# Turning q and k by TensorE's transposes in the first eight steps of a fused RetNet and MLP kernel, with the heads paired anew and w_in's rows loaded to match

## The chip, the cores and the metric

The kernel runs on one core of a Trainium2 chip. Its time is what the device records for one execution, in microseconds (us), and a lower one is better. Medians of several executions are given. A comparison of two kernels uses runs on the same chip, taken in turns, and only runs in the fast state; all runs below were in it, but for m1_probe, which ran once and has no known state. Engines are written as in the profile: PE is TensorE's matmuls, PEld its weight loads, DVE is VectorE, ACT is ScalarE, POOL is GpSimd, SP is SyncE. The DMA engines are 16.

The kernel before takes 682.3 to 688.7 us from one execution to another. So effects below 2 us need the intervals that are given with them.

## The reference

```python
# attention: batch 4, 8 heads, 768 tokens, head_dim 64, float32
for t in range(S):
    state = gamma[None, :, None, None] * state + einsum('bhd,bhe->bhde', k[:, :, t], v[:, :, t])
    y[:, :, t] = scale * einsum('bhd,bhde->bhe', q[:, :, t], state)
x = y.transpose(0, 2, 1, 3).reshape(3072, 512)      # feature = head * 64 + d
h = x @ w_in                                        # 512 x 2048
g = h * (1.0 / (1.0 + exp(-1.702 * h)))
out = g @ w_out                                     # 2048 x 512
```

The weights reach the kernel as 64-bit floats and are narrowed on the chip: ScalarE and VectorE read both words of each.

## The kernel before

The recurrence runs in chunks of 64 tokens for two batches at a time: 24 steps. The first eight stand in a hand-written order between the narrowing of the weights and the first layer of the MLP. The other 16 turn q and k on VectorE and are not touched in substance. Here is what the change touches, cut.

```python
# loads of w_in: P = 128 partitions, two 512 KB transfers per pair of blocks
w1v = moe_w_in.bitcast(U32).rearrange("(c p) (f two) -> p c f two", p=P, two=2)
SRC = [w1v[:, 2 * h:2 * h + 2, 2 * p * P:2 * (p + 1) * P] for p in range(NP) for h in range(2)] + ...
def fetch(i):
    x = raw(i).rearrange("p (n two) -> p n two", two=2)
    pin(sp.dma_start(x.rearrange("p (c f) two -> p c f two", c=2) if i < NFF else x, SRC[i]))

def turn(j):                        # q and k of step j: from token rows to head_dim rows
    ...
    for n in (1, 0) if j else (0, 1):
        for s in range(HP):         # HP = 4
            for r in range(2):      # head HP * r + s goes to half r of the partitions
                pe.matmul(p[n][HALF[r], s, :], x[n][:, HP * r + s, :], ident, start=True, stop=True)

def attend(j, f=None):              # quarter-array matmuls (64 rows x 64 columns), four at a time
    ...                             # k q^T -> pa; k^T v -> pa; state and attention -> py

def aged(f):                        # state times the decay of a whole chunk, on ScalarE
    for s in range(HP):
        pin(act.activation(new[:, :, s], old[:, :, s], AF.Copy, scale=whole[:, s:s + 1]))

def lay_whole():                    # whole[half r, s] = decay of head HP * r + s
    for r in range(2):
        pin(pool.dma_start(whole[HALF[r]], bass.AP(..., offset=... + H + HP * r, ap=[[0, D], [1, HP]])))
```

The kernel lays four quarter-array matmuls (64 rows x 64 columns) side by side in the array, so that the two that share rows have different columns (in the trace, four of them begin within 20 ns at 21.24 us, and the next four 59 ns after the first). To keep that, a head's half of the partitions as an input (r) and as an output (o) are chosen independently of each other. Before, r parted the heads into 0 to 3 and 4 to 7, and o into even and odd ones. Even and odd heads in the halves of the output make chunk c of x's features the rows 128c to 128c + 127 of w_in, which are contiguous.

## Time and profile before

| | before |
|---|---|
| time, median of the first 4 runs | 684.62 us (684.2 to 684.91) |
| TensorE busy | 668.9 of 683.3 us |
| turns | 256 matmul records, 1.90 us each turn |
| w_in's transfers | 16 of 512 KB, 6.0 us from issue to landing in the median |

The prediction shows the page's main lines; these are further ones. First the view by windows: each row gives a stretch in us, the busy time of each engine with its instruction count, then TensorE's granted clock, the mean share of the DMA engines and GB/s.

```profile
10.00:20.00 10.00, 8.21 (x188) 5.96 (x187) 8.15 (x14) 9.11 (x29) 2.83 (x4) 1.00 0.89 231
20.00:30.00 10.00, 8.61 (x189) 7.43 (x186) 9.35 (x13) 8.00 (x26) 0.00 (x0) 1.00 0.87 227
...
40.00:50.00 10.00, 10.00 (x110) 8.61 (x104) 8.96 (x12) 7.39 (x22) 0.00 (x0) 1.00 0.91 241
```

The clock is whole (1.00; its record begins at 10.8 us, and the view counts time without a record as whole). The view of waits of the first 100 us (total, times, longest):

```profile
ACT W L189 <- DMA W<-in_moe_w_in_dram: 10.5, 4, 5.7
...
ACT W L189 <- DMA G<-in_moe_w_in_dram: 1.7, 2, 1.0
```

(Part of w_in passes through a buffer that the program calls G.) ScalarE's timeline has the wait for the whole decay, and the view of that tile the time of its load:

```profile
18.76 1.28 ACT L322 ACTIVATE state<-state,whole 128x128 f32<-128x128 f32 x4 [0.44 <-DMA whole<-in_col_decay_dram]
```

```profile
DMA to landing us min/median/max: 3.5/3.6/3.6
```

Last, the row of the page for the queue that brings instructions (transfers, MB, share), and two lines of TensorE's timeline.

```profile
24.72 0.45 PE L265 MATMUL pa<-G 64*64 64x64 f32 x12 [1.35 <-issue]
...
85.97 10.46 PE L396 MATMUL ph<-W,W 128*128 128x512 f32 x24
```

The 1.35 us without a cause was the one such wait above 0.4 us here, and it was not looked into before predicting. The group at 85.97 is the first of the second quarter of the MLP's first layer; its start will serve as a milestone.

### The profile page before, as it was taken

Reading aid. Unit: us, or ns where it says so; the run is one execution under the profiler, and the core shown is the slowest. Engines: PE = TensorE matmul, PEld = TensorE weight load, DVE = VectorE, ACT = ScalarE, POOL = GpSimd, SP = SyncE. Lnnn points to the kernel's source line nnn. Section 1 sums busy time; section 2 is a strip of 40 time slices with the busy share of each in tenths; the row PEclk is TensorE's granted clock in tenths of the full one; section 3 lists DMA queues with packets and bytes.
Section 4 is the critical chain, followed back from the end, with each engine's and each line's share of the span. In section 5 each row is a group of like instructions: output and inputs, shape, how many; then the busy total and the mean of one; then the engine's idle time right before and its main releaser. Section 6 shows DMA issues by size and latency. Waiting matters only on the chain.

```text
span 683.3 us, 13882 instructions
## 1 busy us (share of the span) xinstructions
PE 668.9 (98%) x5830; PEld 558.7 (82%) x5830; DVE 367.1 (54%) x514; ACT 151.1 (22%) x293; POOL 125.5 (18%) x116
## 2 busy tenths in 40 slices
PE   6899999999999999999999999999999999999997
PEld 4788854757788888888888888888888888888886
DVE  3899994989811843443752453563345372345241
ACT  5775423221000001332000332000333000233000
POOL 3000000000467414000434000244100243000030
PEclk9999999999999999999999999999999999999999
DMA  7887631332222224301333310313310210000001
GB/s 179 231 236 212 177 130 62 123 84 35 49 34 64 61 45 103 58 1 16 73 57 84 54 32 9 75 31 89 72 40 3 50 45 32 16 0 1 16 0 47
DMA packets 140334, 46.55 MB, mean 68 GB/s; under 512 B 131824, under 2 KB 132848, under 8 KB 140272
## 3 DMA queue, kind: packets, MB, share of 16 engines
q1 hardware_dynamic: 136352, 39.10, 24.9%
q0 software_dynamic: 1760, 5.26, 2.0%
q10 hardware_dynamic: 2160, 1.31, 0.6%
q8 instruction: 46, 0.75, 0.5%
q14 instruction: 16, 0.13, 0.1%
HBM read 39.33 MB, written 6.29 MB: 67 GB/s over the span
## 4 chain that ended last, share of the span: by engine, by line
PE 84%; DVE 7%; SPq 5%; DMA 1%; issue 1%; ACT 1%; ACTq 0%
PE pd L503 37%; PE px L435 16%; PE py L435 12%; PE ph L384 6%; SPq L140 4%; PE ph L396 4%; PE pa L265 2%; PE pt L232 2%; PE py L290 2%; PE pa L275 2%; PE py L284 2%; SPq L126 1%; PE pd L488 1%; DVE G L425 1%; DMA W<-in_moe_w_out_dram 1%
## 5 line engine op out<-in xcount | busy, mean ns | idle before, releaser
L503 PE MATMUL pd<-W,G 128*128 128x256 f32 x1088 | 240.5, 381 | 1.3 <-issue 0.9
L503 PEld LDWEIGHTS pd<-W,G 128*128 128x128 f32 x1088 | 205.2, 190 | 30.4 <-DVE G L426 1.2
L435 PE MATMUL px<-X,W 128*128 128x256 f32 x512 | 119.0, 379 | 0.0
L435 PEld LDWEIGHTS px<-X,W 128*128 128x128 f32 x512 | 97.3, 190 | 13.2
L435 PE MATMUL py<-X,W 128*128 128x256 f32 x384 | 90.7, 379 | 0.0
L435 PEld LDWEIGHTS py<-X,W 128*128 128x128 f32 x384 | 73.0, 190 | 9.9
L384 PE MATMUL ph<-X,W 128*128 128x256 f32 x256 | 57.6, 382 | 0.0
L396 PE MATMUL ph<-W,W 128*128 128x512 f32 x128 | 55.6, 592 | 0.0
L384 PEld LDWEIGHTS ph<-X,W 128*128 128x128 f32 x256 | 48.1, 190 | 8.2 <-issue 1.0
L256 POOL TENSOR_TENSOR kd<-kn_in,cold 128x512 f32<-128x512 f32 x14 | 16.4, 1173 | 187.5 <-PE pa L275 163.8
L396 PEld LDWEIGHTS ph<-W,W 128*128 128x128 f32 x128 | 24.3, 190 | 28.9 <-issue 28.4
L427 POOL TENSOR_TENSOR G<-G 128x512 f32<-128x512 f32 x20 | 29.5, 1480 | 91.8 <-DVE G L426 91.8
L356 ACT ACTIVATE sg<-G 128x512 f32<-128x512 f32 x48 | 30.3, 630 | 51.3 <-DVE G L445 31.0
L361 DVE TENSOR_TENSOR G<-G,sg 128x512 f32<-128x512 f32 x48 | 33.5, 699 | 13.7 <-ACT sg L356 13.7
L296 DVE TENSOR_TENSOR at<-pa,mask 128x512 f32<-128x512 f32 x16 | 11.0, 686 | 54.7 <-PE pa L275 54.7
L324 POOL TENSOR_TENSOR state<-state,whole 128x512 f32<-128x512 f32 x13 | 13.5, 1038 | 128.1 <-DVE state L332 127.9
L503 PE MATMUL pd<-W,W 128*128 128x256 f32 x160 | 35.8, 381 | 1.0 <-DVE W L426 1.0
L503 PEld LDWEIGHTS pd<-W,W 128*128 128x128 f32 x160 | 30.2, 190 | 6.3 <-DVE W L426 1.8
L475 ACT ACTIVATE u<-pd 128x512 f32<-128x512 f32 x6 | 3.6, 597 | 137.3 <-PE pd L503 137.3
L356 ACT ACTIVATE sg<-ph 128x512 f32<-128x512 f32 x32 | 18.9, 595 | 66.2 <-PE ph L396 32.9
L480 POOL DMA_DIRECT2D out_dram<-o x20 | 14.9, 745 | 91.4 <-DVE o L479 91.4
L445 DVE TENSOR_TENSOR G<-py,p 128x512 f32<-128x512 f32 x16 | 11.1, 692 | 38.1 <-PE py L435 38.1
(112 smaller groups left out, 676.0 us busy)
## 6 DMA issues: line engine op xcount, KB each, us to landing
W<-in_moe_w_in_dram SPq DMA_DIRECT2D x12, 512.0 KB, 6.1
v_in<-in_v_dram SPq DMA_DIRECT2D x48, 128.0 KB, 3.3
kn_in<-in_k_dram SPq DMA_DIRECT2D x42, 128.0 KB, 3.4
W<-in_moe_w_out_dram SPq DMA_DIRECT2D x10, 512.0 KB, 4.4
out_dram<-o POOLq DMA_DIRECT2D x20, 256.0 KB, 2.7
q_sq<-in_q_dram SPq DMA_DIRECT2D x256, 16.0 KB, 1.9
k_sq<-in_k_dram SPq DMA_DIRECT2D x256, 16.0 KB, 1.9
G<-in_moe_w_out_dram SPq DMA_DIRECT2D x6, 512.0 KB, 3.9
```

The source lines that it names most:

```text
L140: tc.keep_in_program_order(sp.dma_start(t[r0:r0 + C4, :, n], src[b + n * C4 // D, h0:h0 + HP, t0:t0 + C4, d0:d0 + C4] .rearrange("h p d -> ...
L232: pe.matmul(p[n][HALF[r], s, :], x[n][:, HP * r + s, :], ident, start=True, stop=True)
L256: pool.tensor_mul(KD[j], x, d.to_broadcast([P, H, D]))
L265: pe.matmul(pa[HALF[i], r, 0, s, :], KT[j][HALF[r], s, HALF[i]], QT[j][HALF[r], s, HALF[i]], start=True, stop=True)
L356: pin(act.activation(s, h, AF.Sigmoid, scale=1.702))
L361: pin(dve.tensor_mul(g, h[:, i], s[:, i]))
L384: pe.matmul(h[:, ab], w, X[:, 2 * th + c // 2, c % 2, :], start=(ab == 0 and c == 0), stop=(c == 3), skip_group_check=True)
L396: pe.matmul(h, w, X1[:, c // 2:4:2, c % 2, :], start=(c == 0), stop=(c == 3))
L427: pool.tensor_sub(a[1], a[1], a[0])
L435: pe.matmul(acc[:, u, :], W1[:, 2 * d + u, sa, c, :], X[:, sb, c, :], start=(start and u == 0 and c == 0), stop=(stop and c == 1), skip_gr ...
L480: (pool if m < NB - 1 else act).dma_start(rows[th, e], o)
L503: pe.matmul(p0[:, n, :], g1(m, p, sa)[:, n * P:(n + 1) * P], W2[:, sb, p, :], start=(new and p == 0 and n == 0), stop=(last and p == NP - ...
```

## The change

The intent is to halve TensorE's time for the turns of the first eight steps: one transpose of a 128 x 128 tile takes the place of two matmuls with 64 rows of result. The two heads of a tile are neighbours in memory, 2s and 2s + 1. Thus r now parts even and odd heads, o has to part 0 to 3 and 4 to 7, and the state, the mask, the row decay and the outputs follow. A chunk of x's features then has 64 rows of w_in from each half of the heads, 256 rows apart. The author loads each half of the partitions by a transfer of its own. The core of the diff:

```diff
-                    for r in range(2):
-                        pe.matmul(p[n][HALF[r], s, :], x[n][:, HP * r + s, :], ident, start=True, stop=True)
+                    pe.transpose(p[n][:, s, :], x[n][:, 2 * s:2 * s + 2, :].rearrange("p r d -> p (r d)"), ident)
...
-    w1v = moe_w_in.bitcast(U32).rearrange("(c p) (f two) -> p c f two", p=P, two=2)
+    w1v = moe_w_in.bitcast(U32).rearrange("(o c d) (f two) -> o d c f two", o=2, d=D, two=2)
...
-        x = raw(i).rearrange("p (n two) -> p n two", two=2)
-        pin(sp.dma_start(x.rearrange("p (c f) two -> p c f two", c=2) if i < NFF else x, SRC[i]))
+        if i < NFF:
+            f = slice(i // 2 * 2 * P, (i // 2 + 1) * 2 * P)
+            for o in range(2) if i < 2 else [i % 2]:
+                x, c = (raw(i), slice(2 * i, 2 * i + 2)) if i < 2 else (raw(i - i % 2, 2), slice(0, HP))
+                pin(sp.dma_start(x[HALF[o]].rearrange("p (c f two) -> p c f two", two=2, f=2 * P), w1v[o][:, c, f]))
...
-                        pe.matmul(pa[HALF[r], i, 1, s, :], kd[HALF[i], HP * r + s, :], vn[HALF[i], HP * r + s, :],
+                        pe.matmul(pa[HALF[r], i, 1, s, :], kd[HALF[i], 2 * s + r, :], vn[HALF[i], 2 * s + r, :],
...
-                            pe.matmul(py[HALF[o], r, 1, i, s2 * D:(s2 + 1) * D], old[HALF[r], i, 2 * s2 + o, :],
-                                      qt[HALF[r], 2 * s2 + o, HALF[i]], start=True, stop=True)
+                            pe.matmul(py[HALF[o], r, 1, i, s2 * D:(s2 + 1) * D], old[HALF[r], i, 2 * o + s2, :],
+                                      qt[HALF[r], 2 * o + s2, HALF[i]], start=True, stop=True)
...   (mask, row decay, outputs, gathers of q and k: the same instructions with other strides)
-                whole[HALF[r]], bass.AP(tensor=col_decay.tensor, offset=col_decay.offset + (D - 1) * W + H + HP * r,
-                                        ap=[[0, D], [1, HP]])))
+                whole[HALF[r]], bass.AP(tensor=col_decay.tensor, offset=col_decay.offset + (D - 1) * W + H + r,
+                                        ap=[[0, D], [2, HP]])))
```

More of the change, by code (lines that the diff above doesn't have):

```diff
@@ L103 @@
     state = [const.tile([P, 2, HP, D], F32, name=f"state{i}") for i in range(2)]
+    HALF = [slice(i * D, (i + 1) * D) for i in range(2)]
     ordered = [True]
@@ L136, in load @@
                 for r0 in range(0, P, C4):
-                    d0, h0 = r0 % D, r0 // D * HP
+                    d0, r = r0 % D, r0 // D
                     for n in range(P // C4):
@@ L140, in load @@
                         tc.keep_in_program_order(sp.dma_start(
-                            t[r0:r0 + C4, :, n], src[b + n * C4 // D, h0:h0 + HP, t0:t0 + C4, d0:d0 + C4]
+                            t[r0:r0 + C4, :, n], src[b + n * C4 // D, r:H:2, t0:t0 + C4, d0:d0 + C4]
                             .rearrange("h p d -> p h d")))
@@ L153 @@
             for r in (W2[:, 4], W2[:, 5], G[:, 6:8].rearrange("p a s t -> p a (s t)"))]
-    SRC = [w1v[:, 2 * h:2 * h + 2, 2 * p * P:2 * (p + 1) * P] for p in range(NP) for h in range(2)] \
-        + [w2v[:, f] for f in range(NFF)]
     def raw(i, n=1):
@@ L161, in fetch @@
     def fetch(i):
-        x = raw(i).rearrange("p (n two) -> p n two", two=2)
-        pin(sp.dma_start(x.rearrange("p (c f) two -> p c f two", c=2) if i < NFF else x, SRC[i]))
+        if i < NFF:
[3 more added lines that the diff above has]
+                pin(sp.dma_start(x[HALF[o]].rearrange("p (c f two) -> p c f two", two=2, f=2 * P), w1v[o][:, c, f]))
+        else:
+            pin(sp.dma_start(raw(i).rearrange("p (n two) -> p n two", two=2), w2v[:, i - NFF]))
     class Narrow:
@@ L209 @@
     QT, KT, KD, AT, TURNED, PA, PU, PY, SHARE = [{} for _ in range(9)]
-    HALF = [slice(i * D, (i + 1) * D) for i in range(2)]
     TWO = [(i, r) for i in range(2) for r in range(2)]
@@ L288, in attend @@
                     for i, o in TWO:
-                        s = 2 * s2 + o
-                        pe.matmul(py[HALF[o], i, 0, r, s2 * D:(s2 + 1) * D], vn[HALF[i], HP * r + s, :],
+                        s = 2 * o + s2
+                        pe.matmul(py[HALF[o], i, 0, s2, r * D:(r + 1) * D], vn[HALF[i], 2 * s + r, :],
                                   a[HALF[i], r, s, :], start=True, stop=True)
@@ L298, in by_state @@
     def by_state(f):
-        SHARE[f] = tmp = two.tile([P, 2, 2, P], F32, name="tmp", bufs=1)
-        pin(dve.tensor_mul(tmp, PY[f][:, :, 1].rearrange("p r i t -> p i r t"),
-                           rowd.rearrange("p (r s) t -> p r (s t)", r=2)[:, None].to_broadcast([P, 2, 2, P])))
+        SHARE[f] = tmp = two.tile([P, 2, 2, 2, D], F32, name="tmp", bufs=1)
+        pin(dve.tensor_mul(tmp, PY[f][:, :, 1].rearrange("p r i (s t) -> p i s r t", t=D),
+                           rowd.rearrange("p (s r) t -> p s r t", r=2)[:, None].to_broadcast([P, 2, 2, 2, D])))
     def output(f):
@@ L307, in output @@
         x = X1 if f // CB == 1 else X
-        x = x[:, 2 * th:2 * th + 2].rearrange("p r s (i t) -> p (r s) i t", i=2)[:, :, :, t0:t0 + D]
-        by = "p i r (s t) -> p (r s) i t"
-        y = PY.pop(f)[:, :, 0].rearrange(by, t=D)
+        x = x[:, 2 * th:2 * th + 2].rearrange("p s r (i t) -> p (s r) i t", i=2)[:, :, :, t0:t0 + D]
+        y = PY.pop(f)[:, :, 0].rearrange("p i s (r t) -> p (s r) i t", t=D)
         if c:
-            pin(dve.tensor_add(x, y, SHARE.pop(f).rearrange(by, t=D)))
+            pin(dve.tensor_add(x, y, SHARE.pop(f).rearrange("p i s r t -> p (s r) i t")))
         else:
@@ L569, in lay_rowd @@
         for o in range(2):
-            pin(act.activation(rowd[HALF[o]], products["rows"][HALF[o], o:H:2, :], AF.Copy))
+            pin(act.activation(rowd[HALF[o]], products["rows"][HALF[o], HP * o:HP * (o + 1), :], AF.Copy))
     def lay_whole():
@@ L585 @@
         "table": lambda: pin(act.activation(first, first, AF.Sigmoid)),
-        "mask": lambda: pin(dve.tensor_mul(m3, products["rows"], cold[:, 0:H, None].to_broadcast([P, H, D]))),
+        "mask": lambda: pin(dve.tensor_mul(mask, products["rows"].rearrange("p (s r) t -> p r s t", r=2),
+                                           cold[:, 0:H].rearrange("p (s r) -> p r s", r=2)[:, :, :, None]
+                                           .to_broadcast([P, 2, HP, D]))),
         "causal": causal, "rows": rows,
```

## The prediction

> **What bounds the kernel now.** I read the page of the kernel before first: its engine shares, its slices and its chain.

> ```profile
> span 683.3 us, 13882 instructions
> PE 668.9 (98%) x5830; PEld 558.7 (82%) x5830; DVE 367.1 (54%) x514; ACT 151.1 (22%) x293; POOL 125.5 (18%) x116
> ...
> PE   6899999999999999999999999999999999999997
> ...
> DVE  3899994989811843443752453563345372345241
> ...
> DMA  7887631332222224301333310313310210000001
> ...
> PE 84%; DVE 7%; SPq 5%; DMA 1%; issue 1%; ACT 1%; ACTq 0%
> PE pd L503 37%; PE px L435 16%; PE py L435 12%; PE ph L384 6%; SPq L140 4%; PE ph L396 4%; PE pa L265 2%; PE pt L232 2%; PE py L290 2%; PE pa L275 2%; PE py L284 2%; SPq L126 1%; PE pd L488 1%; DVE G L425 1%; DMA W<-in_moe_w_out_dram 1%
> ```

> TensorE carries 84% of the chain, and the row that the change goes after, pt L232, holds 2% of it. One slice is 17.1 us. In the first five, VectorE (DVE) is at 80 to 90% as well after the start and the DMA engines at 60 to 80%: the head of the kernel has three nearly full resources. After it only TensorE is full. So I looked at the head alone. The view by tile gives the instructions that turn q and k of the first eight steps:

> ```profile
> L232 PEld LDWEIGHTS pt<-ident,q_in x128: 137/137/231, 7.3 to 71.2; 128*64 128x64 f32 x128
> L232 PE MATMUL pt<-ident,q_in x128: 272/273/476, 7.4 to 71.3; 128*64 128x128 f32 x128
> ```

> There are 128 for q and as many for k: eight steps, 16 matmuls of the program each, two records per matmul. Then the timeline of the head (start, duration, engine, and in brackets the idle time before and who ended it), where I sought, for each stretch of TensorE work, when the VectorE result that it needs was ready:

> ```profile
> 28.75 1.09 PE L232 MATMUL pt<-ident,kn_in 128*64 128x128 f32 x16
> ...
> 29.68 1.04 PE L232 MATMUL pt<-ident,q_in 128*64 128x128 f32 x16
> ...
> 30.65 0.69 PE L275 MATMUL pa<-v_in,G 64*64 64x64 f32 x32
> ...
> 33.15 1.17 ACT L189 ACTIVATE W<-W 128x1024 f32<-128x1024 f32 x1 [1.78 <-DMA W<-in_moe_w_in_dram]
> ...
> 39.52 1.23 DVE L204 TENSOR_TENSOR W<-W 128x1024 f32<-128x1024 f32 x1
> ...
> 41.95 7.17 PE L384 MATMUL ph<-X,W 128*128 128x256 f32 x32
> ...
> 49.87 0.68 DVE L296 TENSOR_TENSOR G<-pa,mask 128x512 f32<-128x512 f32 x1
> ```

> One turn begins at 28.75 and the next work at 30.65: 1.90 us per turn, 8 pairs of matmuls at 237 ns (the two of a pair write different halves of the partitions and run together). TensorE has no wait between 25 and 182 us. But VectorE is close behind. The weights of the third pair are finished at 39.52 + 1.23 = 40.75, and TensorE begins with them at 41.95: 1.2 us of slack. Their narrowing began when a load landed (ScalarE waited 1.78 us for it), not when TensorE allowed it. The mask of step 4 is done at 50.55 and the next step, which needs that buffer, starts at 51.57 in the TensorE timeline: 1.0 us.

> [...]48 records of 512 columns (24 matmuls) take 20.6 us (99.72 to 120.33), 858 ns each, 1.68 ns per column. [...]190 ns for 128 columns and 137 for 64, a difference of 53 ns[...]

> **The change part by part.**
> Turns: 16 matmuls in 8 concurrent pairs become 8 transposes on the whole array. [...]I put one transpose at 107 to 120 ns if loads overlap the previous matmul as they do everywhere in this trace. 8 x 0.118 = 0.95 us per turn (estimate), against 1.90: 0.95 us less. Seven turns lie between 13.6 and 71.6 us: 6.65 us of TensorE work. The first (7.4 to 11.0) [...]it may lose 1.8, but ScalarE follows it at once with a load it waited for until 9.44 and two copies, so about 0.5 us comes through.
> Pairing anew: the mask, the row decay, the state and the outputs get other strides with the same instructions, shapes and counts (DVE 0.69 us each, 128x512). The two TensorE halves of each step keep their rows and columns of the array and their count. Zero.
> w_in's rows: the same bytes in runs of 2 KB, but each transfer fills 64 partitions with four runs instead of 128 with two. Zero by bytes. For the first block each of the two transfers becomes two: two more issues at about 0.6 us (SP took 0.63 for one) at 2.5 and 9.6 us. The whole-decay load fetches single elements instead of runs of four; it was waited for by 0.44 us at 18.76, so 0 to 0.5 us.
> Later steps: the gathers of q and k take every other head, in the same 128-byte runs and the same count. Zero.

> **What of 6.65 us reaches the end.** After 96 us no turn is left, so TensorE's lead can only shrink. If the landings of the weights are pinned where they are, the lead at 51.57 is capped at 1.0 us by the mask of step 4 (it stands behind a weight block in VectorE's fixed order, and that one began on a landing). The last turn, at 69.6, adds 0.95: 1.95 us. The next cap is the block that TensorE first uses at 96.27 in its timeline; VectorE ends it at 93.74 + 1.23 = 94.97, with 0.66 us of its own idle time before it at 87.9 that a faster TensorE removes: 1.3 + 0.66 = 2.0 us. So **1.9 us is the gain with pinned landings**. If landings move too (loads are issued when turns free the q and k buffers, so some will), VectorE can shed its idle time between 30 and 52 us: 0.93 + 0.38 + 0.87 + 0.53 = 2.7 us by its waits in the timeline. Then about 1.95 + 2.2 (a little of the 2.7 is start-up that ScalarE paces) = 4.1 us. DMA engines at 81 to 91% between 20 and 50 us in the view by windows leave only little room, so I take a point nearer the first: 2.8 us. From 96 on the lead should stay: ScalarE and VectorE wait for TensorE from 102 to 115 (3.76 us before the block at 115.31), the chain through VectorE and the q_sq gathers (140 to 175) starts from there and moves with it, and from 188 us to the end TensorE waits for nothing over 1 us.

> **Rivals.** (1) TensorE is the only bound and all of it counts: 6.65 + 0.5, 677.7 us. For: no TensorE wait for 157 us. Against: the slacks of 1.0 to 1.3 us. (2) VectorE takes over at once and DMA paces it: 1 to 2 us, 683. For: VectorE 90% or more in that stretch; against: waits of VectorE for TensorE and ScalarE in it. (3) The transpose gains nothing: [...]685 to 687. [...] (4) Half-partition weight loads land later, which delays VectorE, already the follower: each 1 us later costs up to 1 us, 684 to 686. For: ScalarE waits 12 us in all for w_in; against: bytes and run lengths are the same.

> **Range and chances.** 684.82 - 2.8 = 682.0 us. Low end: rival 1 in part, 679.5 (5.3 us gained). High end: rival 3 or 4 in part, 684.5. Two per cent is 13.7 us, twice all the work removed, so faster by that is nearly excluded, 0.01; slower by it would need a new stall repeated in each step, 0.01.

> **What would show it.** Right: 64 transposes in the pt rows, some 0.95 us per turn; the first-layer matmuls that began at 53.6 begin 1 to 2.5 us earlier, TensorE shows new waits on VectorE between 38 and 97 us that add up to 3 to 5 us, and from 100 us on everything is shifted by the same 2 to 4 us. VectorE's busy time stays at 367 us. Wrong: turns still at 1.9 us (rival 3); longer ScalarE waits on w_in (rival 4); a shift that reaches 6 us (rival 1); or a later stage, such as the sums at 181 to 188, where TensorE waits for VectorE, giving the lead back.

The 107 to 120 ns for one transpose, and with them the 0.118 and 0.95 us, are the author's estimate: the trace before holds no transpose. What it holds are weight loads, 190 ns for 128 columns and 137 for 64. At 53 ns for 64 columns more, an estimated 106 ns of a load go with 128 columns.

## More of the kernel before

`issue` means that the wait has no cause the profile shows.

```profile
q8 instruction: 46, 0.75, 0.5%
```

## The result, and the profile after

| | before | after |
|---|---|---|
| time, median of 4 runs | 684.62 us (684.2 to 684.91) | 692.91 us (692.05 to 694.99) |
| ratio | | 1.0126 (1.0102 to 1.015) |
| time, median in a later round (g3) | 684.44 us (11 runs) | 693.8 us (5 runs) |
| ratio there | | 1.013 (1.0104 to 1.0155) |

A ratio is the mean time of one kernel's runs over that of the other's runs of the same rounds. So it isn't quite the ratio of the medians quoted. The range in brackets is a 95% interval.

The changed kernel is 1.3% slower. That is inside "within 2%", but 8 us above the kernel before and outside the range of 679.5 to 684.5. From its page:

```profile
span 693.0 us, 13497 instructions
...
PE 669.6 (97%) x5638; PEld 557.1 (80%) x5638; DVE 366.5 (53%) x514; ACT 149.8 (22%) x293; POOL 125.6 (18%) x116
...
PE   7688999999999999999999999999999999999998
...
DVE  4578986799941473444373345374345383344241
...
PEclk9898999999999999999999999999999999999999
DMA  8899664132222223310323320233320220000001
...
q8 instruction: 44, 0.72, 0.4%
```

Slices 2 to 4 (17 us each) are where the loss is: TensorE is less full in them than before, the clock falls in the second and the fourth, and the DMA engines are busier than before in the third and the fourth. The turns themselves did as expected (the view of the tile, then TensorE's timeline):

```profile
L237 PE MATMUL pt<-ident,q_in x32: 272/273/445, 6.4 to 80.4; 128*128 128x128 f32 x32
```

```profile
32.64 0.60 PE L237 MATMUL pt<-ident,kn_in 128*128 128x128 f32 x4
33.07 0.60 PE L237 MATMUL pt<-ident,q_in 128*128 128x128 f32 x4
33.60 0.69 PE L280 MATMUL pa<-v_in,G 64*64 64x64 f32 x32
```

There are 32 transposes for q and as many for k. A turn takes from 32.64 to 33.60, 0.96 us. One record lasts 273 ns, but the records overlap: the four at 33.07 begin 0.43 us after the four at 32.64. But the loads have changed. The windows as before:

```profile
10.00:20.00 10.00, 7.60 (x139) 5.18 (x138) 8.35 (x15) 6.80 (x23) 2.99 (x4) 0.99 0.78 142
20.00:30.00 10.00, 5.59 (x140) 5.08 (x141) 3.51 (x6) 4.69 (x12) 0.00 (x0) 0.67 0.88 184
...
40.00:50.00 10.00, 8.19 (x132) 6.94 (x131) 8.47 (x11) 4.29 (x15) 0.00 (x0) 1.00 0.92 196
```

At the same DMA share the engines move a fifth less: 184 for 227 GB/s at 0.88, 196 for 241 at 0.92. From 20 to 30 us VectorE works 3.51 us instead of 9.35, and the mean clock is 0.67. The waits, and ScalarE's and TensorE's lines that stand out:

```profile
ACT W L196 <- DMA W<-in_moe_w_in_dram: 16.6, 5, 5.9
...
ACT state L326 <- DMA whole<-in_col_decay_dram: 5.5, 1, 5.5
ACT W L196 <- DMA G<-in_moe_w_in_dram: 4.7, 2, 2.9
```

```profile
23.12 1.28 ACT L326 ACTIVATE state<-state,whole 128x128 f32<-128x128 f32 x4 [5.54 <-DMA whole<-in_col_decay_dram]
```

```profile
DMA to landing us min/median/max: 6.7/7.9/9.2
```

```profile
23.41 1.09 PE L237 MATMUL pt<-ident,kn_in 128*128 128x128 f32 x4 [5.44 <-DMA kn_in<-in_k_dram]
...
87.45 0.33 PE L295 MATMUL py<-G,v_in 64*64 64x64 f32 x4 [1.28 <-issue]
...
97.17 10.46 PE L400 MATMUL ph<-W,W 128*128 128x512 f32 x24
```

ScalarE waits 21.3 us on w_in (16.6 + 4.7) where it waited 12.2 (10.5 + 1.7), and 5.5 us on the load of the whole decay, which takes 7.9 us where it took 3.6. TensorE's own wait there, 5.44 us before 23.41, is put down to a load of k. The milestone comes at 97.17, 11.2 us late, and the end is 9.7 us late in these two profiles. So the loss is complete before 100 us, and the rest of the kernel follows it.

The trace has each packet of each transfer. Two kinds changed:

```
packets                         before            after
2048 bytes (w_in, 4096 of them) median 84 ns      median 153 ns
64 bytes (whole decay, 32)      median 32 ns      median 988 ns
```

w_in's packets thus take 37.6 us of the time of each of the 16 DMA engines instead of 26.6 (their sum over 16). The transfers as wholes grow less: their median from issue to landing goes from 6.0 to 7.0 us.

### The profile page after: what moved, and what is told of

Same layout as the page of the kernel before. It is cut to its first block, busy times and chain, and to the rows that moved or that the text cites. A ratio compares the mean times of both kernels' runs of the same rounds, so it can differ in the third digit from the quotient of the medians.

```text
span 693.0 us, 13497 instructions
## 1 busy us (share of the span) xinstructions
PE 669.6 (97%) x5638; PEld 557.1 (80%) x5638; DVE 366.5 (53%) x514; ACT 149.8 (22%) x293; POOL 125.6 (18%) x116
## 4 chain that ended last, share of the span: by engine, by line
PE 80%; DVE 8%; SPq 6%; DMA 4%; issue 1%; ACT 0%; ACTq 0%
PE pd L507 36%; PE px L439 16%; PE py L439 12%; PE ph L388 5%; SPq L142 4%; PE ph L400 3%; PE pa L270 2%; PE pa L280 2%; PE py L295 2%; PE py L289 1%; DMA kn_in<-in_k_dram 1%; SPq L128 1%; DMA W<-in_moe_w_in_dram 1%; PE pd L492 1%; DMA v_in<-in_v_dram 1%
## 5 line engine op out<-in xcount | busy, mean ns | idle before, releaser
L365 DVE TENSOR_TENSOR G<-G,sg 128x512 f32<-128x512 f32 x48 | 33.0, 688 | 13.7 <-ACT sg L360 13.7
L449 DVE TENSOR_TENSOR G<-py,p 128x512 f32<-128x512 f32 x16 | 11.1, 691 | 38.1 <-PE py L439 38.1
```

Of the source, the lines that this page charges most:

```text
L365: pin(dve.tensor_mul(g, h[:, i], s[:, i]))
```

## The experiments

Three causes are put to the test. **A**: w_in's transfers into half of the partitions are slower. **B**: the load of the whole decay, now in single elements of 4 bytes, is slower and holds ScalarE up. **C**, formed on the way: something at TensorE itself takes the rest. The main rival to A and B is that the new pairing of the heads, or the shorter turns themselves, cost the time by changing the order in which buffers come free. The letters of the expectations differ: in those of e2 to e4, C is the load of the whole decay and B is that rival; in f1, D and E are the clock and the waits at TensorE; in h1 to h3, F is the C of here.

Kernels that are wrong load some rows of w_in or some decays under the wrong feature: the same instructions, bytes and shapes, with wrong values. They only serve to put back one load.

### e2_full_rows: the changed kernel with w_in loaded as before (wrong result)

```diff
-    w1v = moe_w_in.bitcast(U32).rearrange("(o c d) (f two) -> o d c f two", o=2, d=D, two=2)
+    w1v = moe_w_in.bitcast(U32).rearrange("(c p) (f two) -> p c f two", p=P, two=2)
     (and fetch() as in the kernel before)
```

> The changed kernel with w_in loaded again into all 128 partitions at once, two runs of 2 KB each (the rows then don't match the heads: the result is wrong on purpose[...]). Theory A (half-partition loads of w_in slow the transfers, packets of 2 KB at 153 ns instead of 84): packets back at 84 ns, the time falls from 692.9 to 681-685. Rival B (the loss comes from the transposes freeing the q and k buffers earlier, so that more transfers collide): stays at 691-694. Rival C (the single-element load of the decays, waited for 5.5 us at 17.6): loses only part, 688-691.

Measured: 687.26 us, ratio 1.0055 (1.0025 to 1.0084). The packets of 2 KB are back at 84 ns. ScalarE still waits 5.1 us for the whole decay. So some 0.7 of the 1.3 percentage points go with w_in's load. The time lies between the forecasts of the two single causes (w_in alone 681 to 685, the decay alone 688 to 691): neither holds by itself.

### e3_half_rows: the kernel before with w_in loaded by halves (wrong result)

```diff
-    w1v = moe_w_in.bitcast(U32).rearrange("(c p) (f two) -> p c f two", p=P, two=2)
+    w1v = moe_w_in.bitcast(U32).rearrange("(o c d) (f two) -> o d c f two", o=2, d=D, two=2)
     (and fetch() as in the changed kernel)
```

> The kernel before with only w_in's loads changed to half the partitions with four runs of 2 KB (wrong result on purpose). Theory A: 692-698, as the loss without the turns' gain; 2 KB packets near 150 ns. Rivals B and C: 684-686.

Measured: 688.76 us, ratio 1.006 (1.0036 to 1.0084), with packets of 2 KB at 154 ns. This single part, in a kernel whose turns and pairs are untouched, costs 4 us, less than the 692 to 698 us that A had forecast. That rules out, for this part, that the pairing is the cause. One thing was not foreseen: TensorE's instructions are those of the kernel before, and yet its waits without a cause grew, from 1.35 us once to

```profile
25.21 0.69 PE L270 MATMUL pa<-G 64*64 64x64 f32 x12 [3.04 <-issue]
...
49.16 3.83 PE L389 MATMUL ph<-X,W 128*128 128x256 f32 x17 [1.62 <-issue]
```

and half clock is recorded from 25.2 to 28.6 us. So not all of the 4 us need be waits for w_in itself; how much is of which kind stays open.

### e4_whole_runs: the changed kernel with the decay loaded in runs of four (wrong result)

```diff
-    ... offset=col_decay.offset + (D - 1) * W + H + r,       ap=[[0, D], [2, HP]]
+    ... offset=col_decay.offset + (D - 1) * W + H + HP * r,  ap=[[0, D], [1, HP]]
```

> The changed kernel with the load of the decays (whole) in runs of four again (wrong values on purpose). Theory A: 690-693, for the other late landings (k at 23.4, w_in) are within a microsecond of this one. Rival C: 684-688.

Measured: 688.94 us, ratio 1.007 (1.0047 to 1.0092). No wait on the decay is left among ScalarE's. The time is again between the two forecasts (690 to 693 and 684 to 688).

### e5_full_rows_whole_runs: both loads as before (wrong result)

The edit is that of e2 and e4 together.

> Both loads undone in the changed kernel (wrong result on purpose): what is left is the transposes and the pairing. As predicted blind for the turns: 680.7-683. If the turns' gain is lost elsewhere: 684-686; if TensorE's saving counted in full: 678.

Measured: 684.81 us, ratio 1.0007 (0.9983 to 1.0031). With both loads undone, only the turns and the pairing are left of the change, and this takes as long as the kernel before. Two things follow. Within the interval, some 2 us either way, A and B together explain the whole loss against the kernel before. But the gain that the prediction worked out, 2.8 us, isn't there either. TensorE's timeline of this run:

```profile
23.12 0.27 PE L285 MATMUL py<-G,state 64*64 64x64 f32 x2 [2.17 <-issue]
...
25.43 6.30 PE L384 MATMUL ph<-X,W 128*128 128x256 f32 x16 [0.69 <-DVE X L312]
...
77.95 0.33 PE L291 MATMUL py<-G,v_in 64*64 64x64 f32 x4 [1.48 <-issue]
```

The waits have no cause in the profile: 2.17 and 1.48 us, where the kernel before had 1.35 once. And the group of 16 matmuls at 25.43 takes 6.30 us. The same group takes 3.72 us at full clock (in the changed kernel, at 29.08). The trace records half clock from 23.9 to 30.7 us.

### f1_first3_ordinary: e5 with turns 0 to 2 by ordinary matmuls (wrong result as in e5)

```diff
+                    for r in range(2) if j < 3 else ():
+                        pe.matmul(p[n][HALF[r], s, :], x[n][:, 2 * s + r, :], ident, start=True, stop=True)
+                    if j >= 3:
-                    pe.transpose(...)
+                        pe.transpose(...)
```

> As e5_full_rows_whole_runs (both loads undone, wrong result on purpose), but the first three turns by ordinary matmuls again, five by transposes. Theory D (transposes and gaps leave TensorE with too little work at the start, so its clock is granted at half for 6.8 us from 24 us on, where the kernel before kept 1.0): no half clock after the start, the first ph group in 3.7 us instead of 6.3, time 681-683. Rival E (instruction waits marked issue, 2.2 and 1.5 us in e5, take the gain): 683.5-685.5 with such waits still there.

Measured: 683.38 us, ratio 1.0001 (0.9979 to 1.0022). Half clock is down to 24.7 to 28.1 us, but waits of kind issue stay, now of 1.52 us at 24.57, 0.71 at 33.42 and 1.29 at 56.90. The time is inside e5's interval: inconclusive, and what brings the clock down is not shown.

### f4_two_queues: w_in's upper halves issued by GpSimd (correct)

```diff
-                pin(sp.dma_start(x[HALF[o]]...
+                pin((sp, pool)[o].dma_start(x[HALF[o]]...
```

> The changed kernel (correct result) with the transfers of w_in's upper 64 partitions issued by GpSimd, the lower by SyncE[...]. Theory A[...]: packets of 2 KB between 85 and 120 ns, 688-691. If half-sized destinations are slow as such: 150 ns, 692-695.

Measured: 695.19 us, ratio 1.0167 (1.015 to 1.0183), a miss: theory A had been expected to give 688 to 691. The 2 KB packets of SP's queue have a median of 135 ns, and the halves land after 6.5 us in the median. Two halves in two queues don't add up to one whole transfer here.

### f5_whole_runs_correct: the decay loaded in runs of eight, every other one used (correct)

```diff
-    whole = const.tile([P, HP], F32, name="whole")
+    whole8 = const.tile([P, H], F32, name="whole")
+    whole = whole8[:, 0:H:2]
...
-                                        ap=[[0, D], [2, HP]])))
+                                        ap=[[0, D], [1, H]])))
```

> The changed kernel with a correct result and the decays loaded as runs of eight values, every other one used. As e4_whole_runs, 687.5-690; ScalarE waits under 1 us for whole instead of 5.5.

Measured: 688.69 us, ratio 1.0085 (1.0065 to 1.0106), against 1.0126 with the single elements. This part of the loss can be mended by loading more than is needed.

### f7_turns_from3: the kernel before with transposes in turns 3 to 7 alone (correct)

Here the heads keep their old pairs, and q and k of these steps are loaded in pair order instead, by twice as many transfers of 64 KB.

```diff
+                for r in range(2) if paired else ():
+                    keep(engine.dma_start(to[:, r:H:2], x[:, HP * r:HP * (r + 1)]))
```

> The kernel before, correct, with only the turns of steps 3 to 7 by transposes; their q and k are loaded in pair order by twice as many transfers (20 more issues of 0.6 us); w_in, decays, pairing as before. Theory: 5 x 1.0 us off TensorE, 1.5-3 us of it kept by the slacks: 681-682.5. Rival: the added issues delay the loads, 684-686.

Measured: 689.02 us, ratio 1.0081 (1.0062 to 1.01), a miss. ScalarE's wait on w_in rises from 10.5 to 15.7 us with w_in's own transfers unchanged, and from 1.7 to 4.2 us for the part of it that goes to buffer G. The added transfers stand in the same queue; that they are the cause was forecast as the rival, but not tested apart. This way around the new pairing costs 5.5 us itself.

### h1_shifted: e5 with 120 TensorE instructions ahead of the first turn (wrong result as in e5)

```diff
+    def pad():      # 30 short matmuls into a tile that nobody reads: 120 TensorE instructions
+        for _ in range(30):
+            pe.matmul(idle[0:32, 0:32], ident[:, 0:32], ident[:, 0:32], start=True, stop=True)
...
-        k0 table q0 warm turn0 ...
+        k0 table q0 warm pad turn0 ...
```

> As e5_full_rows_whole_runs (both loads undone, wrong result on purpose), with 30 short matmuls (120 TensorE instructions) ahead of the first turn, into a tile nobody reads. Theory F: TensorE's instructions come in blocks of 256; all the waits marked issue in the traces so far stand at the instructions 193 + 256 k[...], after which the clock may be halved. The transposes take instructions and time out of the turns, and so moved the block ends into the dense steps. Shifted by 120 they should fall into or near the ph groups: no issue wait over 0.5 us before 100 us, no half clock after the start, 679.5-682. Rival: waits and half clock come from the transposes as such: 684-686.

Measured: 682.45 us, ratio 0.9961 (0.9933 to 0.9989), the first that is faster than the kernel before: 2.7 us. From its TensorE timeline:

```profile
24.43 3.72 PE L384 MATMUL ph<-X,W 128*128 128x256 f32 x16 [0.81 <-DVE X L312]
...
83.14 10.46 PE L396 MATMUL ph<-W,W 128*128 128x512 f32 x24
```

No wait of kind issue of 0.4 us or more of the matmuls is left in the first 100 us (the block end at number 705 lies in a wait for VectorE), half clock is recorded from 18.3 to 21.7 us alone, the group of 16 takes 3.72 us again, and the milestone at 83.14 is 2.8 us earlier than in the kernel before (85.97) and 4.0 earlier than in e5 (87.17). The half clock had been expected to be gone.

The two traces show where the 4.0 us come from. At the end of the group of 16, h1 is 3.6 us ahead (its next turn starts at 27.98, in e5 at 31.56): 1.0 us from the start of the group, 2.6 us from the clock inside it. Some of that is lost again: at the last of the eight turns h1 is 2.1 us ahead. The other 1.9 us come between there and the milestone, where e5 has its wait of 1.48 us.

h1 is not a pure shift, though. With its extra matmuls the clock is also full earlier, at 8.1 us instead of 17.0 in e5. At a group of matmuls at 18 us the two still stand level (18.07 and 18.15), so the earlier clock gave no lead by itself; whether it moved the later stretch of half clock is not known. A shift by 256, which would leave the block ends where they were, was not run.

### h2_before_shifted: the kernel before with 136 instructions ahead (correct)

The edit is that of h1 with 34 short matmuls, on the kernel before.

> The kernel before, correct, with 34 short matmuls (136 instructions) ahead of the first turn. Theory F: block ends move into steps 3, 5 and 7, three issue waits of 1.5 to 3 us, perhaps a half clock: 687-691. Rival: 683.5-685.

Measured: 690.16 us, ratio 1.0067 (1.0039 to 1.0094), as theory C had forecast (687 to 691). The same kind of shift harms the kernel before, and its trace has a wait that wasn't there:

```profile
56.64 0.57 PE L290 MATMUL py<-G,v_in 64*64 64x64 f32 x22 [1.83 <-issue]
```

It stands after number 1985, which is 193 + 7 x 256, with one of 0.73 us after number 1217. They are 2.6 us together, but the 1.35 us of the kernel before are gone, so the waits give 1.2 of the 4.6 us; how the rest comes about wasn't followed up. A shift of the instructions is thus worth several us either way in a kernel whose work is the same; that the block ends are the whole of it is not shown.

### h3_changed_shifted: f5 with 120 instructions ahead (correct)

The edit is that of f5 and of h1.

> The changed kernel, correct, with the decays loaded in runs and the same 30 short matmuls. Theory F with theory A still in force for w_in: 3 to 4 us under f5_whole_runs_correct, 684.5-686.5. Rival: 688-690.

Measured: 686.99 us, ratio 1.0024 (0.9999 to 1.0049), against 1.0085 for f5: some 4.2 us, with a correct result. But the two ran on different chips, and theory C doesn't explain it: the waits of kind issue are longer here than in f5 (2.62 us at 25.00 and 3.27 at 36.48, after numbers 705 and 961, against 1.68 and 0.85). So the decay is mended here with a correct result; the waits for instructions are not, and w_in's halves stay.

### m1_probe: which partitions make the packets slow (the kernel before, with eight more loads near its end; correct)

```diff
+    for lo, n in ((0, 128), (0, 64), (32, 64), (64, 64)) * 2:
+        c = 256 // n
+        tc.keep_in_program_order(sp.dma_start(probe[lo:lo + n, 0:c * 512]...,      # 512 KB each, in runs of 2 KB
+            wv.rearrange("(c p) f -> p c f", p=n)[:, 0:c, 0:512]))
```

> The kernel before, correct, with eight added loads of 512 KB from w_in near its end, one after the other, while the queues are quiet, into partitions 0-127, 0-63, 32-95 and 64-127, twice, in runs of 2 KB. Theory A[...]: 84 ns per packet for 0-127 and for 32-95, near 150 ns for 0-63 and 64-127. Rival (64 partitions with four runs each are slow as such): 150 ns for 32-95 too. The time of the kernel itself is of no interest.

Measured (packets of 2 KB, from the trace, two loads of each kind; one run, 683.19 us):

```
partitions      0-127       0-63         32-95       64-127
median ns       84, 84      128, 153     84, 84      140, 104
```

It isn't the number of partitions, nor the run length or the bytes, which are equal. 64 partitions from 32 on are as fast as 128, while 64 from 0 or from 64 on are slower. The transfers as wholes differ less: 2.4 to 2.6 us from first to last packet for 0-127 and 32-95, 2.7 to 2.9 for the other two. Why these ranges differ is not shown.

### g1_all_partitions: w_in in the new order of rows, with each transfer over all 128 partitions (correct)

One transfer per chunk, 256 KB, whose source steps from one half of the heads to the other in its outermost dimension of 2. It has f5's load of the decay.

```diff
-            for o in range(2) if i < 2 else [i % 2]:
-                ...
+            for c in range(2):
+                pin(sp.dma_start(raw(i)[:, c * F2:(c + 1) * F2],
+                                 bass.AP(tensor=w1u.tensor, offset=...,
+                                         ap=[[HP * D * 2 * DFF, 2], [2 * DFF, D], [1, F2]])))
```

> The changed kernel, result correct, with w_in's rows in the new order but each transfer filling all 128 partitions with one 2 KB run (256 KB, so twice as many transfers of half the size), and the whole decay in contiguous runs of 8. Theory (half-partition destinations and single-element runs cost some 7 us, issues little): packets of 2 KB back at a median of 84 ns, ratio to the kernel before 1.000 to 1.004, as the wrong-result kernel with both loads undone had 1.0007. Rival (what costs is the number and smallness of the transfers, or the new order of the rows itself): ratio 1.007 to 1.012, and ScalarE waits on w_in stay near 21 us.

Measured: 812.14 us, ratio 1.1859 (1.1826 to 1.1893). Both theories missed. The view of its waits and a row of its page:

```profile
ACT W L199 <- DMA W<-in_moe_w_in_dram: 92.2, 6, 19.3
```

```profile
DMA  3232221242232222222320324202233012000001
```

The packets of 2 KB are back at a median of 84 ns, as A has it. But just two of them at a time were under way for 155 of the 176 us in which any was, and never more than four, against up to 16 and more in the kernel before. The outermost dimension of these transfers is 2; of w_in's in the kernel before it is 128, in the changed kernel 64. That this is what leaves two packets under way is the author's reading, not tested apart. Putting the dimension of 64 outermost would need a destination that steps whole partitions in an inner dimension.

### g2_all_partitions_shifted: g1 with 120 instructions ahead (correct)

> The same with 30 short matmuls (120 TensorE instructions) ahead of the first turn, result correct. Theory of the instruction blocks: 2 to 3 us less than g1_all_partitions, ratio to the kernel before 0.996 to 1.001, no wait of kind issue above 1 us on TensorE in the first 100 us. Rival (the shift's gain was luck of one kernel): same as g1_all_partitions.

Measured: 811.91 us, ratio 1.1857 (1.1827 to 1.1887), no gain on g1 where 2 to 3 us had been forecast. It says nothing on theory C: g1 has waits of ScalarE on w_in of up to 19.3 us, behind which a gain of 2 to 3 us at TensorE can go unseen.

### g3_changed_again: the changed kernel on the same chip as g1, g2 and g4

> The changed kernel itself, on the same chip as its mends. Expected 1.0126 again, between 1.010 and 1.015, that is 691.5 to 694.5 us if the kernel before takes 684.6. Rival: the first measurement fell on an unlucky chip, and it is 1.007 to 1.010 here; the parts of the loss that were found would then have to be scaled down.

Measured: 693.8 us, ratio 1.013 (1.0104 to 1.0155), as the first time. ScalarE again waited 5.0 us for the decay and 17.5 us for w_in. The packets of 2 KB had a median of 155 ns. The loss comes back in another round.

### g4_before_shifted_5: the kernel before with 20 instructions ahead (correct)

The edit is that of h1 with 5 short matmuls.

> The kernel before with 5 short matmuls (20 TensorE instructions) ahead of the first turn, result correct. Replaying the recorded block times with the shift gives some 1.5 us less: ratio 0.998 (0.996 to 1.000), the 1.35 us wait of kind issue at 24.7 gone or below 0.7 us. Rival: the waits only move, ratio 1.000 to 1.003.

Measured: 684.03 us, ratio 0.9985 (0.9961 to 1.001), not told apart from no change. The wait that was to go stayed, after number 705 as before:

```profile
24.51 0.57 PE L265 MATMUL pa<-G 64*64 64x64 f32 x22 [1.28 <-issue]
```

So the place of the waits is known, but replaying recorded block times was too coarse to foretell the effect of a shift as small as this. No correct version here is shown to beat the kernel before.

## Why the prediction was wrong

The ratios give these differences, in us at 684 us. Each ratio has an uncertainty of 1.5 to 2 us, a difference of two has more, and the runs are of several chips:

| step | from | cost |
|---|---|---|
| w_in by halves (A) | changed kernel - e2: 8.8 - 3.8; e4 - e5: 4.8 - 0.5; e3 alone: 4.1 | 4.1 to 5.0 |
| decay in single elements (B) | changed kernel - e4: 8.8 - 4.8; e2 - e5: 3.8 - 0.5 | 3.3 to 4.0 |
| shift of the instructions (C, argued) | e5 - h1: 0.5 + 2.7 | 3.2 |
| what is left of the change with the shift (h1) | 684 x (0.9961 - 1) | -2.7 |

The measured loss is 8.8 (the mean of the two measurements, 1.0126 and 1.013). That the parts add up to it (7.9 to 9.5) proves nothing, since each is a difference between neighbours on the way from the changed kernel to h1. Only e3 measures a part by itself. Nor are the parts independent: A's runs have longer waits for instructions as well (e3: 3.04 and 1.62 us).

**Right.** The turns: 64 transposes, 0.96 us for each turn by the timeline, against 0.95 predicted. VectorE's busy time: 366.5 us, as good as unchanged. That from 100 us on the shift stays about the same: 11.2 us at the milestone, 9.7 at the end. Only its sign was wrong. Its own sign for rival 4, longer waits of ScalarE on w_in, came true: 12.2 to 21.3 us.

**Luck, or open.** The 2.7 us of h1 (0.8 to 4.6 by its interval) look like the 2.8 predicted, but they contain the 1.35 us wait of the kernel before, which h1 hasn't got, and the shift. No run has the shorter turns alone with loads and block ends as before; so whether the caps of 1.0 to 2.0 us from which the prediction worked out its 2.8 hold isn't shown. In e5, without the shift, no gain is seen (1.0007).

**The step "Zero by bytes" failed.** It is the largest term. The prediction saw that each transfer fills 64 partitions instead of 128, and held that bytes and run lengths decide. The same bytes took 153 instead of 84 ns per packet. m1_probe shows that it's a matter of which partitions a transfer fills: 84 ns for 0 to 127 and for 32 to 95, 104 to 153 for 0 to 63 and 64 to 127. The reason isn't shown. The DMA engines were already busy for 0.81 to 0.91 of just this stretch (10 to 50 us), and ScalarE, with VectorE and TensorE behind it, waited for w_in 21.3 us instead of 12.2. Put back alone into the kernel before, this change of load cost 4.1 us (e3). Rival 4 named the effect, but put the time with it at 684 to 686 us, where it alone (e3) gave 688.76. Its argument against ("bytes and run lengths are the same") is the one that fell.

**The step "0 to 0.5 us" for the whole decay failed.** It counted the load as hidden but for 0.44 us of wait and didn't ask what single elements do to its own time. Its packets went from 32 to 988 ns, it landed after 7.9 instead of 3.6 us, and ScalarE stood for 5.5 us in place of 0.44. The load of 2 KB was small enough to be overlooked; it cost 3.3 to 4.0 us.

**A term was missing: TensorE's supply of instructions.** The prediction took "TensorE has no wait between 25 and 182 us" and the 1.35 us wait just before as given. That wait was the sign of a block of 256 instructions coming in late. Removing 48 of 64 instructions from each turn moved all block ends. That these waits are for instructions is shown by their places and by the landings of the transfers; that the lost gain of e5 is due to them is in part argued (h1 and h2 for it, h3 not). In the changed kernel waits stand at 87.45 (1.28 us) and 95.88 (0.53). In e5 they are 2.17 and 1.48 us, and half clock follows for 6.8 us. Half clock is recorded in stretches of 3.4 us or a multiple of it (19.9 to 26.7 and 57.4 to 64.2 in the changed kernel, 23.3 to 33.6 in e2), and in the kernel before not at all from 10.8 to 683.2 us. But what brings the clock down isn't shown. h1 has half clock from 18.3 to 21.7 us without any wait of kind issue. The shorter turns themselves are a rival: the kernels with transposes in the first turns and no extra matmuls have full clock on record only from 13.6 to 17.0 us on (g1, which waits for w_in, aside), those with ordinary first turns from 7.1 to 11.1 us on. They can't be all of it, for e3 has half clock without a transpose. Nor is it shown what sets the start of a block's fetch (in e5 it came 3.45 us after number 193, elsewhere much sooner or later).

## What to carry to other kernels

Before re-ordering heads or rows for the sake of one engine, write down for each transfer whose pattern changes: which partitions it spans, its contiguous run, and its outermost dimension. Packets of equal bytes took 1.8 times as long here for the first (153 for 84 ns; whole transfers 1.15 to 1.2 times, by m1_probe and the landings) and 30 times for the second (988 for 32 ns, a packet of 16 single elements). For the third, w_in's transfers with an outermost dimension of 2 kept just two packets under way for most of their time, in a kernel that was 19% slower (g1). In a kernel with stretches of very short matmuls, a wait of TensorE with no visible cause may be instruction supply. Here it waited up to 4.6 us (e2) after number 193 + 256k, and a shift of 120 to 136 instructions was worth -3.2 us (e5 to h1) or +4.6 us (h2), of which the waits are only a part. So count instructions to such a wait, and test it by a shift before crediting a gain or a loss to the work itself. And read a sequence's cost from the starts of its records: the FP32 transposes here have records of 273 ns, but follow each other every 109 ns (four in 0.43 us).
